# Scan and mixture of experts on one core: the first three chunks emitted whole before the weights, weight loads in ScalarE's DMA queue

## The chip, the cores and the metric

The kernel runs on one core of one Trainium2 chip. A core has TensorE (matmuls, PE in the profile; its weight loads are PEld), VectorE (DVE), ScalarE (ACT), GpSimd (POOL) and SyncE (SP, which here only issues DMAs), and 16 DMA engines that move data between HBM and the on-chip memory. Each engine works through its own stream of instructions in order; a "q" behind the engine's name marks what its sequencer does, such as issuing a DMA. The metric is the time of one execution on the device in microseconds (us), taken as the median over runs.

## The reference

A gated linear recurrence runs along each sequence, and its output goes through a mixture of experts in which each token takes one expert:

```
sig = 1 / (1 + exp(-f_logit));  f = lower_bound + (1 - lower_bound) * sig
h = f[:, t] * h + (1 - f[:, t]) * x[:, t];  y[:, t] = h        # t = 0 .. S-1
logits = y @ w_gate;   e_idx = argmax(logits);   gate_w = softmax(logits)[e_idx]
eom = 1 / (1 + exp(-(y @ w_output_gate)))
out = gate_w * eom[e_idx] * (relu(y @ w1[e_idx]) @ w2[e_idx])
```

Batch 4, sequence 5056 (20224 tokens), width 256, 8 experts, inner width 1024, float32 in and out.

## The kernel before

*Chunks.* The tokens go through the recurrence in 40 chunks of 512, channels on the partitions. `load_chunk` brings a chunk's two inputs (512 KB each) in by DMA from SP (L250, L251). `chunk` is a generator: tanh on ACT (L265), a product on DVE (L269), a scale on ACT (L274), the scan on DVE (L280), squares on ACT (L287) and a small matmul (L291) for a power-of-two scale (`pow2`), the scaled result split into two f16 halves (ACT L310, DVE L314), four DMA transposes from SP to token rows (`turn`, L307), the gate matmuls, about two dozen small DVE operations for expert, position and factor (the last is L430), and four indirect DMAs on POOL (L433) that scatter the rows into a scratch in HBM, sorted by expert. A bare `yield` ends a segment of a chunk; there are 16 of them. Within a segment, `yield SMALL` and `yield BIG` let `together` interleave the DVE work of several generators. Chunks 0 and 3 borrow memory of the weight tables of the last two experts (`lent`), the others share two buffers. `loading` wraps the generator and, at its fifth segment, issues the load of the next chunk.

*Weights.* Each of 8 experts has two halves (w1 and w2): 16 half-experts j = 0 to 15. `prep_load(j)` brings one in by two DMAs of 512 KB (L566); a matmul with itself (`prep_gram`, L578), DVE's norm (L585), a small matmul and `pow2` give a scale; ACT makes the high f16 half (`prep_hi`, L614) and DVE the low one (`prep_lo`, L619). Eight buffers hold four half-experts; the load for a later j waits until its buffer is free.

*Early tiles.* While weights are prepared, tiles of 128 tokens already run through experts that are ready. `plan_first` makes a table for one tile per expert once 3 chunks are done, and again at 5 (`EARLY`). `early(j)`, called twice a step, gathers such a tile (`gather`: a DMA transpose of the rows L630 and a small DMA L633, both on SP) and runs half of it: first matmuls (L719 to L721), relu on ACT (L723), low half on DVE (L730), second matmuls (L739 to L741), scaling on ACT (L750) and the indirect DMA of the output (L754). An expert's tile is gathered at step j = 2e + 1 at the earliest, and one tile is in work at a time.

*Order.* The loop over j = -2 to 15 emits all this; `step(k)` runs k pumps on average. A `pump` begins a chunk when `prog["tick"]` has run down, then runs one segment of each live chunk together with the step's other work and one plan. The pumps of a step are FILL = 12 for j = -2 and -1, PUMPS0 = 3 for j = 0 to 2, and PUMPS = 2.25 after. Chunks 0, 1 and 2 begin 3 pumps apart (`GAPS`), the later ones 8 (`PERIOD`). After j = 15 a closing loop (DRAIN = 1.25 pumps an iteration) runs until all 16 early tiles are through. Then come the main tiles of 256 tokens (`experts`, L675 to L677 and L706 to L708), four pumps each; a main tile copies its expert's weights on DVE (L657, L663), and its table comes from `plan` (L486 to L555). Behind 64 such tiles come single blocks of 128 tokens.
The streams of DVE, ACT, PE and POOL up to the first main tile are put in order by the compiler's scheduler, which takes the order of emission as priority; SP's stream, and every stream behind that point (`ordered`), stays as emitted.

Of the kernel before, what the change touches and what calls it, by code (L numbers as in the profile page):

```python
# [26 lines left out]
TX = 8  # L27
PERIOD = 8
PUMPS = 2.25
FILL = 12  # L30
MORE = (18, 21)
EARLY = (3, 5)
LOADAT = 5
GAPS = (3, 3)
PUMPS0 = 3.0
TURN = 3
XB = 2
# [3 lines left out]
LEAD = 2  # L41
# [4 lines left out]
def raw(ins):  # L46
    return getattr(ins, "ins", ins)
# [3 lines left out]
def tile_scan_moe(  # L51
# [10 lines left out]
    nc = tc.nc  # L62
    P = 128
# [8 lines left out]
    NCH = -(-N // CH)  # L72
    R = N + P
    FREE = E * R
# [3 lines left out]
    WH = WE // 2  # L78
    QH = WH // 2
# [4 lines left out]
    def sure(tokens):  # L84

        return max(0, -(-(tokens - len(EARLY) * E * P - E * 255) // 256))
# [8 lines left out]
    scr = dp.tile([E * R + P, RW], I16, name="scr")  # L95
# [8 lines left out]
        out=tri, in_=ones, compare_op=ALU.is_gt, fill=0.0, base=0, pattern=[[1, P]], channel_multiplier=-1  # L104
# [48 lines left out]
    def together(tasks):  # L153

        at = {id(g): (g, next(g, None)) for g in tasks}
        last = None
        while True:
            todo = [(g, kind) for g, kind in at.values() if kind]
            if not todo:
                return  # L160
            best = [x for x in todo if x[1] == SMALL and x[0] is not last]
            best = best or [x for x in todo if x[1] == BIG] or todo
            g = best[0][0]
            last = g if best[0][1] == SMALL else None
            del at[id(g)]
            at[id(g)] = (g, next(g, None))

    def alone(g):
# [12 lines left out]
        out=gsq, in0=wgf, scalar=1.0, in1=wgf, op0=ALU.mult, op1=ALU.mult, accum_out=gss  # L181
# [9 lines left out]
        out=wgs[:, :, 1, :], in0=wgc, scalar=gsc, in1=wgs[:, :, 0, :], op0=ALU.mult, op1=ALU.subtract  # L191
# [3 lines left out]
    fresh = []  # L195

    def apart(ins, group, keep=()):
        tc.declare_no_dep(raw(ins), group=group, keep=[raw(k) for k in keep], reason="rows apart")
        tc.add_to_no_dep_group(group, raw(ins))
# [8 lines left out]
    padt = cp.tile([P, RW], I16, name="padt")  # L208
    nc.gpsimd.memset(padt, 0)
    nc.gpsimd.iota(padt[:, CM + 2 : CM + 4].bitcast(I32), pattern=[[0, 1]], base=N, channel_multiplier=0)  # L210
    fresh.append(nc.sync.dma_start(out=scr[FREE : FREE + P, :], in_=padt))
    apart(fresh[0], "scr")
    row2 = [cp.tile([P, NB, RW], I16, name=f"rows{i}") for i in range(2)]

    top1 = w1f[:, (E - 1) * 2 * WH : E * 2 * WH]
# [16 lines left out]
    def beside(n=None):  # L232
        for _ in range(len(queue) if n is None else min(n, len(queue))):
            f, a = queue.pop(0)
            f(*a)
# [5 lines left out]
    def load_chunk(c):  # L241
        t0 = c * CH
        n = min(CH, N - t0)
        if c in lent:
            fx = lent[c].bitcast(F32).rearrange("p (i k n) -> p i k n", i=2, k=KD)
            ft, xt = fx[:, 0], fx[:, 1]
        else:
            ft = p1.tile([P, KD, CH], F32, tag="ft", name="ft", bufs=XB)
            xt = p1.tile([P, KD, CH], F32, tag="xt", name="xt", bufs=XB)
        nc.sync.dma_start(out=ft[:, :, 0:n], in_=fv_in[:, :, t0 : t0 + n])  # L250
        nc.sync.dma_start(out=xt[:, :, 0:n], in_=xv_in[:, :, t0 : t0 + n])  # L251
        loaded[c] = (xt, ft)
# [309 lines left out]
    def prep_load(j):  # L562
        ws = []
        for i in range(2):
            w = wp.tile([P, QH], F32, tag="w", name="w")
            nc.sync.dma_start(out=w, in_=wT[j // 2][:, j % 2 * WH + i * QH : j % 2 * WH + (i + 1) * QH])  # L566
            ws.append(w)
        half[j] = dict(w=ws)

# [46 lines left out]
    def prep_lo(j, z):  # L616
        (h, r), (l, _) = parts(j, 0, z), parts(j, 1, z)
        yield BIG
        nc.vector.scalar_tensor_tensor(out=l, in0=r, scalar=half[j]["sc"], in1=h, op0=ALU.mult, op1=ALU.subtract)  # L619
# [141 lines left out]
    prog = {"begun": 0, "tick": 0, "done": 0, "left": 0.0, "planned": 0, "final": False, "got": 0, "rounds": 0}  # L761
# [7 lines left out]
    def loading(c):  # L769

        at = 0
        for kind in chunk(c):
            if not kind:
                at += 1
                if at == LOADAT and EARLY[0] <= c + 1 < NCH:
                    load_chunk(c + 1)
            yield kind

    def plans(need):
        c = prog["done"]  # L780
        if prog["final"]:
            return
        while prog["rounds"] < len(EARLY) and c >= min(EARLY[prog["rounds"]], NCH):
            prog["rounds"] += 1
            planning.append(plan_first())
        k = sure(min(N, c * CH)) - prog["planned"]
        if k >= need or (k > 0 and c == NCH):
            prog["planned"] += k
            planning.append(plan(k, 2, False))
        if c == NCH:  # L790
            prog["final"] = True
            planning.append(plan(tail, 1, True))

    def pump(tasks, need):

        beside()
        if prog["tick"] <= 0 and prog["begun"] < NCH:
            live.append(loading(prog["begun"]))
            prog["tick"] = GAPS[prog["begun"]] if prog["begun"] < len(GAPS) else PERIOD
            prog["begun"] += 1  # L800
        prog["tick"] -= 1
        mine = planning[:1]
        del planning[:1]
        together([*live, *tasks, *mine])
        for g in [g for g in live if g.gi_frame is None]:
            live.remove(g)
            prog["done"] += 1
        plans(need)

    def step(k, tasks, need=PLAN):  # L810
        prog["left"] += k
        if prog["left"] < 1.0:
            together(tasks)
        while prog["left"] >= 1.0:
            prog["left"] -= 1.0
            pump(tasks, need)
            tasks = []
# [62 lines left out]
            prep_load(n - 1)  # L880
    for n in range(min(EARLY[0], NCH) - 1, deep):
        prep_load(n)
    for j in range(-2, nh):
        tasks = []
        if 1 <= j < nh + 1 - deep:
            prep_load(j - 1 + deep)
        if 0 <= j + 1 < nh:
            tasks.append(prep_scale(j + 1))
        for z in range(2):
            if 0 <= j:  # L890
                tasks.append(prep_lo(j, z))
            mine, rest = early(j)
            tasks += mine
            step((PUMPS if j >= TURN else PUMPS0 if j >= 0 else FILL) / 2, tasks, LEAD)
            if 0 <= j + 1 < nh:
                prep_hi(j + 1, z)
            rest()
            tasks = []
            if j + 2 < nh:
                if z == 0:  # L900
                    prep_gram(j + 2)
                    tasks.append(prep_norm(j + 2))
                else:
                    prep_sum(j + 2)
# [110 lines left out]
```

## Time and profile before

| | |
|---|---|
| median of 3 runs | 1020.92 us (1020.44 to 1021.68) |
| the profiled execution: its time, its span | 1019.5 us, 1017.8 us |
| busy PE, DVE, ACT, POOL | 917.6 (90%), 886.5 (87%), 511.8 (50%), 378.2 (37%) us |
| first arithmetic on a chunk on DVE | 9.06 us |
| first matmul of an early tile (L719) | 61.5 us |
| last low half of a weight (L619) begins | 149.62 us |
| first matmul of a main tile (L675) | 185.4 us |
| mean granted clock of TensorE | 0.989 |

In a row in order of time the columns are start, duration, engine, line, operation, output <- inputs, shape, count; in brackets stands how long the engine had been idle and what ended that. A row of waits names the waiting engine and line, what it waited for, and total, number and longest of these waits. A row of the table by stages has the stretch, its length, then for each engine its busy time and number of instructions, the granted clock, the DMA engines' share, and GB/s.

### The profile page before, as it was taken

How to read it: one execution, taken by the hardware profiler on the slowest of the kernel's cores; microseconds unless marked ns; L12 is line 12 of the kernel's file. 1: busy time of each engine (PE TensorE's matmuls, PEld its weight loads, DVE VectorE, ACT ScalarE, POOL GpSimd, SP SyncE). 2: the span in 40 equal slices, each digit the busy share in tenths (PEclk: the TensorE clock that was granted, in tenths of full speed). 3: DMA queues.
4: the chain of work that ended last, by engine and by line, in shares of the span. 5: the costliest groups of instructions: out<-in, count | busy, mean ns of one | idle time of the engine just before them, and what ended most of it. 6: DMA issues, size and time to landing. Idle time of an engine off the chain costs nothing. (4 is left out here: it accounts for less than half of the span.)

```text
span 1017.8 us, 27499 instructions
## 1 busy us (share of the span) xinstructions
PE 917.6 (90%) x9775; PEld 822.5 (81%) x9775; DVE 886.5 (87%) x2803; ACT 511.8 (50%) x1075; POOL 378.2 (37%) x378
## 2 busy tenths in 40 slices
PE   2267998899999999999999999999999999999993
PEld 2156987788888888888888888888888888899993
DVE  7889897899999999999999999999999998758771
ACT  5667684554554555545545455455455543333331
POOL 1532334334344443433444434344444344221121
PEclk9999999999999999999999999999999999999997
DMA  8899976755655556456566555565565644321120
GB/s 311 200 305 271 254 179 147 163 154 137 139 136 151 145 136 163 135 136 142 132 141 156 157 147 133 136 139 132 142 154 135 151 91 97 97 54 43 43 55 16
DMA packets 238546, 146.34 MB, mean 144 GB/s; under 512 B 202557, under 2 KB 204223, under 8 KB 238400
## 3 DMA queue, kind: packets, MB, share of 16 engines
q1 hardware_dynamic: 222752, 101.74, 43.5%
q0 software_dynamic: 15360, 42.74, 13.3%
q8 instruction: 80, 1.31, 0.6%
q14 instruction: 66, 0.54, 0.2%
q10 hardware_dynamic: 288, 0.02, 0.0%
HBM read 58.38 MB, written 44.49 MB: 101 GB/s over the span
## 5 line engine op out<-in xcount | busy, mean ns | idle before, releaser
L675 PE MATMUL ph<-xq,w 128*128 128x256 f16 (+1 forms) x1312 | 331.0, 261 | 3.2 <-DMA xq<-scr 2.7
L677 PE MATMUL ph<-xq,w 128*128 128x256 f16 (+1 forms) x1312 | 331.6, 261 | 0.0
L676 PE MATMUL ph<-xq,w 128*128 128x256 f16 (+1 forms) x1312 | 331.3, 261 | 0.0
L706 PE MATMUL py<-w,hh 128*128 128x256 f16 x1168 | 318.0, 272 | 10.4 <-DVE w L663 5.5
L708 PE MATMUL py<-w,hl 128*128 128x256 f16 x1168 | 318.3, 273 | 0.0
L707 PE MATMUL py<-w,hh 128*128 128x256 f16 x1168 | 318.2, 272 | 0.0
L754 POOL DMA_INDIRECT out_dram<-yo,mt x146 | 165.9, 1137 | 298.4 <-ACT yo L750 270.5
L433 POOL DMA_INDIRECT scr<-rows,dst x154 | 178.9, 1162 | 225.3 <-issue 212.5
L680 ACT ACTIVATE hh<-ph 128x512 f16<-128x512 f32 (+1 forms) x328 | 178.7, 545 | 156.9 <-PE ph L677 154.9
L688 DVE SCALAR_TENSOR_TENSOR hl<-ph,hh 128x512 f16<-128x512 f32 (+1 forms) x328 | 204.8, 625 | 10.4 <-ACT hh L680 8.6
L675 PEld LDWEIGHTS <-w 128*128 128x128 f16 x1312 | 128.0, 98 | 16.5 <-DVE xt L269 3.0
L677 PEld LDWEIGHTS <-w 128*128 128x128 f16 x1312 | 128.1, 98 | 12.1
L657 DVE COPY w<-w1s 128x2048 f16 x164 | 114.9, 701 | 26.2 <-PE ph L677 24.7
L676 PEld LDWEIGHTS <-w 128*128 128x128 f16 x1312 | 127.9, 97 | 9.7
L707 PEld LDWEIGHTS <-hh 128*128 128x128 f16 x1168 | 113.9, 98 | 23.2 <-issue 12.7
L708 PEld LDWEIGHTS <-hl 128*128 128x128 f16 x1168 | 113.9, 98 | 13.5
L706 PEld LDWEIGHTS <-hh 128*128 128x128 f16 x1168 | 113.9, 98 | 11.2
L663 DVE COPY w<-w2s 128x2048 f16 x164 | 111.9, 682 | 0.5 <-PE py L708 0.3
L274 ACT ACTIVATE ft<-ft,fb,fa 128x512 f32<-128x512 f32 (+1 forms) x76 | 60.6, 807 | 97.9 <-DVE xt L269 90.1
L310 ACT ACTIVATE ft<-xt,sa 128x512 f16<-128x512 f32 (+1 forms) x76 | 50.2, 708 | 104.9 <-DVE li L299 100.7
L280 DVE TENSOR_TENSOR_SCAN xt<-ft,xt 128x512 f32<-128x512 f32 (+4 forms) x78 | 90.9, 1173 | 0.0
L750 ACT ACTIVATE yo<-py,fac 128x256 f32<-128x256 f32 x146 | 61.5, 465 | 26.4 <-PE py L708 22.8
(172 smaller groups left out, 1355.0 us busy)
## 6 DMA issues: line engine op xcount, KB each, us to landing
ft<-in_fT_dram SPq DMA_DIRECT2D x37, 512.0 KB
xt<-in_xT_dram SPq DMA_DIRECT2D x37, 512.0 KB
w<-in_wT_dram SPq DMA_DIRECT2D x32, 512.0 KB
scr<-rows,dst POOLq DMA_INDIRECT x154, 2.8
rows<-ft SPq DMA_TRANSPOSE x152
out_dram<-yo,mt POOLq DMA_INDIRECT x146, 2.4
xq<-scr SPq DMA_TRANSPOSE x99
scr<-padt SPq DMA_DIRECT2D x9, 136.0 KB
```

Source lines behind the costliest of these rows:

```text
L433: ins = nc.gpsimd.indirect_dma_start(out=scr[:, :], out_offset=IOA(ap=dst[:, b : b + 1], axis=0), in_=rows[:, b, :], in_offset=None)
L657: nc.vector.tensor_copy(out=w, in_=w1f[:, ds(T["ev"] * (2 * WH) + h * 2 * QH, 2 * QH)])
L663: nc.vector.tensor_copy(out=w, in_=w2f[:, ds(T["ev"] * (2 * WH) + h * 2 * QH, 2 * QH)])
L675: nc.tensor.matmul(out=o, lhsT=w[:, f, k, 0, :], rhs=T["xh"][:, k, 0:n], start=first, stop=False)
L676: nc.tensor.matmul(out=o, lhsT=w[:, f, k, 0, :], rhs=T["xl"][:, k, 0:n], start=False, stop=False)
L677: nc.tensor.matmul(out=o, lhsT=w[:, f, k, 1, :], rhs=T["xh"][:, k, 0:n], start=False, stop=last)
L680: nc.scalar.activation(hh[:, :, 0:n], ph[:, :, 0:n], AF.Relu)
L688: nc.vector.scalar_tensor_tensor(out=hl[:, :, 0:n], in0=ph[:, :, 0:n], scalar=0.0, in1=hh[:, :, 0:n], op0=ALU.max, op1=ALU.subtract)
L706: nc.tensor.matmul(out=o, lhsT=hh[:, i, c], rhs=w[:, f, 0, :], start=first, stop=False, skip_group_check=True)
L707: nc.tensor.matmul(out=o, lhsT=hh[:, i, c], rhs=w[:, f, 1, :], start=False, stop=False, skip_group_check=True)
L708: nc.tensor.matmul(out=o, lhsT=hl[:, i, c], rhs=w[:, f, 0, :], start=False, stop=last, skip_group_check=True)
L754: ins = nc.gpsimd.indirect_dma_start(out=out[:, :], out_offset=IOA(ap=T["mt"][:, b, 2:4].bitcast(I32), axis=0), in_=T["yo"][:, b, :], in_o ...
```

## The change

Four edits. Chunks 0, 1 and 2 are emitted whole, one after the other, before the loop over j; the two steps that ran 12 pumps now run one each, and chunk 3 begins with the first pump. The weight loads are issued from ScalarE's queue instead of SP's. The store of the padding rows goes from the front of SP's queue to behind the first loads. The constants GAPS and FILL go.

```diff
-FILL = 12
-GAPS = (3, 3)
+GAP = 0
...
-    fresh.append(nc.sync.dma_start(out=scr[FREE : FREE + P, :], in_=padt))
-    apart(fresh[0], "scr")
     row2 = [cp.tile([P, NB, RW], I16, name=f"rows{i}") for i in range(2)]
...
             w = wp.tile([P, QH], F32, tag="w", name="w")
-            nc.sync.dma_start(out=w, in_=wT[j // 2][:, j % 2 * WH + i * QH : j % 2 * WH + (i + 1) * QH])
+            nc.scalar.dma_start(out=w, in_=wT[j // 2][:, j % 2 * WH + i * QH : j % 2 * WH + (i + 1) * QH])
...
             live.append(loading(prog["begun"]))
-            prog["tick"] = GAPS[prog["begun"]] if prog["begun"] < len(GAPS) else PERIOD
+            prog["tick"] = PERIOD
             prog["begun"] += 1
...
     for n in range(min(EARLY[0], NCH) - 1, deep):
         prep_load(n)
+    fresh.append(nc.sync.dma_start(out=scr[FREE : FREE + P, :], in_=padt))
+    apart(fresh[0], "scr")
+
+    for n in range(min(EARLY[0], NCH)):
+        prog["begun"] += 1
+        for kind in loading(n):
+            pass
+        prog["done"] += 1
+        plans(LEAD)
+    prog["tick"] = GAP
     for j in range(-2, nh):
...
-            step((PUMPS if j >= TURN else PUMPS0 if j >= 0 else FILL) / 2, tasks, LEAD)
+            step((PUMPS if j >= TURN else PUMPS0 if j >= 0 else 1) / 2, tasks, LEAD)
```

## The prediction

> **What bounds the kernel now.** I read the page, then a table of the engines by stage, then each engine in order of time, then the waits. The page's slices say where time can be had: the middle is full, the first seven slices (25 us each) are not alike.
>
> ```profile
> span 1017.8 us, 27499 instructions
> ...
> DVE  7889897899999999999999999999999998758771
> ```
>
> The table has stages cut at events: first chunk arithmetic (9 us), first matmul of an early tile (61.5), end of weight preparation (151), first main tile (185.4), one-block tiles (899). Columns: PE, PEld, DVE, ACT, POOL busy, granted clock, DMA share, GB/s.
>
> ```profile
> 9.00:41.00 32.00, 11.43 (x137) 9.36 (x136) 30.91 (x127) 22.38 (x47) 5.71 (x5) 1.00 1.05 296
> 41.00:61.50 20.50, 2.90 (x41) 1.90 (x42) 17.36 (x56) 15.11 (x26) 9.28 (x10) 1.00 0.81 237
> 61.50:151.00 89.50, 78.53 (x1101) 73.82 (x1101) 78.07 (x256) 62.01 (x105) 29.41 (x30) 0.98 0.99 254
> 151.00:185.40 34.40, 29.32 (x376) 26.60 (x373) 25.84 (x96) 17.66 (x38) 14.59 (x14) 0.95 0.60 136
> 185.40:899.00 713.60, 693.29 (x6769) 614.50 (x6770) 654.08 (x2092) 354.06 (x764) 293.27 (x278) 1.00 0.56 137
> ```
>
> From 185.4 on PE is 97% busy: that part is PE's and the diff removes no matmul. Before it DVE is 97% busy to 41 us, 85% to 61.5, 87% to 151, beside a DMA share near 1; PE has little to do until 61.5. So the change can only move the moment 185.4, and what moves it is DVE work and queues ahead of it.
>
> **What holds the first early tile.** In time order, SP's queue:
>
> ```profile
> 3.16 0.38 SPq L211 DMA_DIRECT2D scr<-padt  x1
> 3.60 0.42 SPq L250 DMA_DIRECT2D w2s<-in_fT_dram  x1
> ...
> 46.20 5.17 SPq L307 DMA_TRANSPOSE rows<-w1s  x4
> ...
> 52.59 1.69 SPq L566 DMA_DIRECT2D w<-in_wT_dram  x2
> 56.06 1.21 SPq L630 DMA_TRANSPOSE xq<-scr  x1
> ```
> ```profile
> 61.50 0.26 PE L719 MATMUL ph<-xq,w1s 128*128 128x128 f16 x1 [2.92 <-DMA xq<-scr]
> ```
> ```profile
> 9.06 1.29 DVE L269 SCALAR_TENSOR_TENSOR w2s<-w2s 128x512 f32<-128x512 f32 x2 [3.68 <-DMA w2s<-in_xT_dram]
> ...
> 40.68 0.22 DVE L430 TENSOR_SCALAR rows<-fc,xi 128x4 f32<-128x4 f32 x1
> ...
> 149.62 1.28 DVE L619 SCALAR_TENSOR_TENSOR w2s<-w,ws,w2s 128x1024 f16<-128x1024 f32 x1
> ```
> ```profile
> 51.22 0.96 POOL L433 DMA_INDIRECT scr<-rows,dst  x1 [0.30 <-issue]
> ```
> ```profile
> DMA to landing us min/median/max: 2.5/2.9/3.5
> ```
>
> Chunk 2's last DVE instruction is at 40.68, the last of its scatters starts on POOL at 51.22 and lands about 2.9 us after its end (the landing row is L433's), at 55.1; the gather follows at 56.06, behind chunk 3's four transposes and a pair of weight loads on SP, and its rows release PE at 61.50. DVE did the three chunks in 31.8 us, of it some 7.9 on other work (weight half 0: two L619 of 1.28; chunk 3: two scans of 1.28, two L269 of 0.65, and about 1.5 of small ones): **8.0 us of DVE per chunk**.
>
> **The change, by count of the code.** A chunk has 17 segments (16 bare yields and the end); a pump runs one segment of each live chunk. Before: 24 pumps in j = -2 and -1 (FILL 12 twice), chunks 0, 1, 2 begun at pumps 0, 3, 6, chunk 3 at 14, then one each 8; 3 pumps a step for j = 0 to 2, 2.25 after: 62 pumps at the end of j = 15. After: chunks 0 to 2 whole, chunk 3 begun at pump 0, one each 8; 1+1+9+29.25 = 40 pumps at the end of j = 15. Chunk segments emitted by then: before 7x17+16+8 = 143, after 6x17+16+8 = 126. **Exactly one chunk (17 segments) leaves the weight stage**, all of it ahead of j = 2, where the first early tile sits. It is done later, among main tiles.
> The second round of early tiles needs five chunks: pump 38 before (j = 5, gathers at j = 6, 8, ... 14), pump 24 after (j = 8, gathers at j = 10, 12, 14). So **two early tiles move behind j = 15**: the closing loop takes 2x4+3 = 11 iterations before, 2x6+3 = 15 after.
>
> **Costs, step by step.**
>
> *Start.* SP no longer waits for POOL's memsets: the 3.60 load can go some 2.5 us earlier. Against it, eight weight loads sit in ACT's queue ahead of the first tanh.
>
> ```profile
> 1.71 1.28 ACT L265 ACT_TABLE_LOAD   x1 [1.71 <-PEq L1004]
> 7.66 1.15 ACT L265 ACTIVATE w2s<-w2s 128x512 f32<-128x512 f32 x2 [4.67 <-DMA w2s<-in_fT_dram]
> ```
> ```profile
> L566 SPq DMA_DIRECT2D w<-in_wT_dram x32: 328/390/1102, 5.6 to 125.7; - x32
> ```
>
> 8 x 0.39 = 3.1 us (8.8 at the slowest issue) from 1.71, and the table load: tanh can start at 6.1, at worst 11.8, against 7.66. Ends -2 and +4; I take -0.5: by the median issue tanh goes 1.6 earlier, and sharing the engines (rival 4) takes most of that back. The padding rows' own store is needed only by the first gather, 50 us on: nothing.
> The loads now go out from two queues at once, where all moved at 296 GB/s in 9 to 41 us. The Trainium skill, "DMA: Bandwidth & Descriptors", Queues, rings and completion order, says each DMA engine alternates between queue rows packet by packet; Issuing engines are not separate DMA queues adds that a second issuer buys no bandwidth. By that, chunk loads get half the rate at the start; the trace, with one queue, cannot show it (rival 4).
>
> *To the first early tile.* One chunk less: -8.0. The chain agrees: three chunks of DVE from 8.5 us (24 us) with 4 to 7 us of weight work slipped between end at 36 to 40; four scatters and landing (about 8) 44 to 48; gather and landing as now (61.5 - 56.06 = 5.4): 50 to 53.5 instead of 61.5. The ends are -4 (chains of dependent small operations stay uncovered) and -12; I take -8.0. SP's transposes of chunk 3 (5.2 us) and weight loads (1.7) go behind the gather; they are not added, as the scatter landing ends last.
>
> *j = 2 to 15 (89.5 us).* Two tiles less:
>
> ```profile
> L730 DVE SCALAR_TENSOR_TENSOR el<-ph,eh 128x512 f16<-128x512 f32 x32 | 21.8, 686 | 3.2 <-ACT eh L723 3.1
> ...
> L649 DVE TENSOR_SCALAR fac<-mt,cinv 128x1 f32<-128x1 f32 x16 | 3.4, 210 | 8.2 <-DMA mt<-scr 8.1
> ```
> 2 x (2x0.686+0.21) = 3.2 us of DVE, at 87% busy 3.7. SP also loses 24 weight loads (24 x 0.39 = 9.4 us) and their waits:
> ```profile
> SPq L566 <- DVE w1s L619: 3.3, 2, 2.0
> ...
> SPq L566 <- DVE xv L146: 0.3, 1, 0.3
> ```
> These are the longest and the shortest of ten such rows, 12.3 us in all, each a time in which gathers and chunk transposes stood behind a load that waited for a buffer. PE waited for gathers, DVE for their small half (8.1 us, above):
> ```profile
> PE ph L719 <- DMA xq<-scr: 13.0, 7, 3.3
> ```
> I give a third of DVE's 8.1 us, -2.5 (ends 0 and -8). The loads land on ACT, which has 27.5 us free of 89.5: 9.4 us of issue fit. I cost that at nothing; what hides it is ACT's idle time, and without it the price is 9.4 + 12.3 = 21.7 us. Behind a waiting load stand ACT's tanh, high halves and relus, and DVE and PE behind those. Sum of the stage: -6.2.
>
> *Closing loop.* 34.4 us for 11 iterations, of which one gather wait:
> ```profile
> 165.10 0.23 PE L719 MATMUL ph<-xq,w1s 128*128 128x128 f16 x1 [3.30 <-DMA xq<-scr]
> ```
> (34.4-3.3)/11 = 2.83 us; PE alone 29.32/11 = 2.67. Four more iterations: +10.5, ends +10 and +12.5 (3.13 each, stall and all).
>
> *Main.* Chunk segments done at its start: 173 before (pump 76), 167 after (pump 59): a third of a chunk more in 713.6 us, nothing on PE but its few gate matmuls. The lead shrinks: between a chunk's last segment and the plan that uses it lie 6 pumps before, 3 after.
> ```profile
> 407.81 0.16 DVE L486 TENSOR_TENSOR pl_n<-cnt,boff 128x8 f32<-128x8 f32 x1
> ...
> 415.58 0.23 DVE L430 TENSOR_SCALAR rows<-fc,xi 128x4 f32<-128x4 f32 x1
> ```
> ```profile
> 420.94 1.49 POOL L433 DMA_INDIRECT scr<-rows,dst  x1 [0.30 <-issue]
> ```
> ```profile
> 433.90 1.26 SPq L630 DMA_TRANSPOSE xq<-scr  x1
> ```
> The period is 22.5 us (8 pumps of 2.8). The gather comes 18.3 us after L430; the rows have landed at 420.94+1.49+2.9 = 425.3, after 9.7. Three pumps less: 9.9. Just enough; 0, at worst +3.
>
> **Sum:** -0.5 -8.0 -6.2 +10.5 = -4.2 us. The profiled execution took 1019.5 (span 1017.8 and 1.7 around it): 1015.3; the median of the runs stands 1.4 higher, so 1020.9 - 4.2 = **1016.7**.
>
> **Rivals.**
> 1. *Slower: ACT becomes the bound of the weight stage.* Of the 21.7 us that move to its in-order queue more than 6.3 stay uncovered (4.2 gained, and 2.1 more). For: ACT is 74% busy in 41 to 61.5, and one waiting load holds all kinds of work. Against: 32.9 us free on ACT from 41 to 151. At half uncovered, +10.8: 1027.5; at the point where it decides, 1023. Chance 0.17.
> 2. *A wash: the stage only trades.* The scheduler, which reorders DVE freely here, fills chunk chains with weights as it does now, so little starts sooner, no SP relief, and an iteration costs 3.13: -0.5-8.0-3.7+12.5 = +0.3: 1021.2. For: PE's work before 185.4 stays the same, tiles only change place. Chance 0.20.
> 3. *A larger gain: SP was the real hold.* All of the 8.1 us of DVE's waits go and the closing loop's 3.3 us stall with them: -4.2 -5.6 -3.3 = -13: 1007.8. For: the gathers' waits above; against: a DMA share of 0.99 delays a gather wherever it is issued. Chance 0.18.
> 4. *The weights crowd the chunk loads.* Chunk 0's 1.05 MB takes 3.5 us alone at 296 GB/s, 7.1 at half rate: +3.5 on the first arithmetic: 1020.2. For: the DMA share is above 1 in 9 to 41 us already; against: SP starts 2.5 us sooner, and DVE has chunks 0 and 1 to do before it needs chunk 2. Chance 0.05. The rule for it is the one of the Trainium skill's page named under *Start*; no row of this trace bears it out or denies it.
>
> The forecast has 0.40. A measurement tells 0.2% (2.0 us) from no change. Faster: 0.37 of the forecast, rival 3, and a little of 2: 0.58. Same: most of 2, part of 4 and of the forecast: 0.21. Slower: 0.21. The range takes in rival 3's end and rival 1's decision point: 1007.5 to 1024; the forecast's own is 1013 to 1019.
>
> **What would show it.** First L719 at 50 to 54 us; last L619 near 136 us; first L675 near 181 us; SP's gathers with no L566 between; ACT's idle time ended by L566 short. Last L619 near 150, with ACT waiting at L566, is rival 1; a gap over 48 us from there to L675, rival 2; x0 later than 9.06, rival 4; waits of L675 for xq through the middle would mean the lead was needed.

## The result, and the profile after

The changed kernel takes 1079.35 us (median of 4 runs, 1077.42 to 1081.33) against 1020.68 us for the kernel before on the same chip (4 runs, 1020.25 to 1021.68): 1.0573 times, 95% interval 1.0552 to 1.0595. It is slower by 58.7 us where the prediction had 4.2 us faster. The profiled execution took 1077.4 us with a span of 1075.7, against 1019.5 and 1017.8. Lines of the changed kernel's code are three lower than before from the dropped lines on (L716 is what L719 was).

The page of the changed kernel (span; busy tenths in 40 slices of 27 us):

```profile
span 1075.7 us, 27421 instructions
...
PE   1218668869999999999999999999999999989993
...
DVE  4668867569999999999999999999999999747772
```

Its table by stages: the same stretch of 9 to 41 us, then cut at its own events as before (first early tile, end of the last low half of a weight, first main tile), and about as long a stretch of main tiles:

```profile
9.00:41.00 32.00, 9.57 (x104) 7.70 (x104) 19.21 (x61) 16.82 (x34) 3.30 (x4) 1.00 0.55 191
41.00:77.30 36.30, 2.56 (x30) 1.52 (x31) 25.86 (x93) 19.60 (x32) 10.19 (x11) 1.00 0.86 213
77.30:171.70 94.40, 69.36 (x955) 65.50 (x955) 73.00 (x250) 57.69 (x95) 23.54 (x22) 0.89 0.88 207
171.70:228.70 57.00, 41.25 (x557) 36.51 (x555) 35.56 (x124) 24.39 (x53) 22.87 (x23) 0.95 0.54 133
228.70:942.00 713.30, 678.80 (x6685) 605.88 (x6685) 659.81 (x2092) 361.02 (x763) 275.14 (x274) 1.00 0.58 136
```

The events in their rows (ACT's queue and first tanh; PE; DVE; PE again):

```profile
1.76 14.73 ACTq L563 DMA_DIRECT2D w<-in_wT_dram  x8
16.52 1.28 ACT L262 ACT_TABLE_LOAD   x1 [16.52 <-DMA ft<-in_fT_dram]
17.82 1.15 ACT L262 ACTIVATE w2s<-w2s 128x512 f32<-128x512 f32 x2
```
```profile
77.28 0.27 PE L716 MATMUL ph<-xq,w1s 128*128 128x128 f16 x1 [12.54 <-DMA xq<-scr]
```
```profile
170.44 1.28 DVE L616 SCALAR_TENSOR_TENSOR w2s<-w,ws,w2s 128x1024 f16<-128x1024 f32 x1
```
```profile
228.66 0.37 PE L672 MATMUL ph<-xq,w 128*128 128x256 f16 x1 [8.04 <-DMA xq<-scr]
```

The first of these rows merges eight issues and the pauses between them. One issue is short (ns: shortest, median, longest):

```profile
L563 ACTq DMA_DIRECT2D w<-in_wT_dram x32: 334/334/513, 1.8 to 134.8; - x32
```

So of the 14.73 us that the first eight take, the larger part is pauses (the longest from 8.2 to 13.9 us), in which ACT's queue does not come to the tanh behind it. The row of the table load names the chunk's input as the releaser, but chunk 0's two inputs had landed by 4.0 and 5.6 us (the ends of their packets in the trace; 6.8 and 8.2 before). It was ACT's queue that held the tanh.

| us | before | after | lost in the stage |
|---|---|---|---|
| first tanh on ACT | 7.7 | 17.8 | 10.2 |
| first early tile | 61.5 | 77.3 | 5.6 |
| last low half of a weight | 149.6 | 170.4 | 5.0 |
| first main tile | 185.4 | 228.7 | 22.4 |
| end of the span | 1017.8 | 1075.7 | 14.6 |

Nothing got faster and no single place holds the loss. The number to see in the table by stages is DVE's: 19.2 us busy of the stretch 9 to 41, where it had 30.9; then 71%, 77% and 62% of the three stages up to the main tiles, where it had 85%, 87% and 75%. DVE's work did shrink in the weight stage (73.0 us instead of 78.1, where 3.2 us less had been counted for two early tiles); its idle time rose from 11.4 to 21.4. PE stands for gathers, in the stretch 60 to 230:

```profile
PE ph L716 <- DMA xq<-scr: 35.0, 5, 12.8
...
PE ph L672 <- DMA xq<-scr: 8.0, 1, 8.0
```

against 13.0 us in seven waits before (60 to 190). And the main tiles have a wait that was not there. The waits of PE in 300 to 900 us, after, and the same wait in the kernel before:

```profile
PE pv L288 <- ACT ft L284: 30.4, 26, 1.6
```
```profile
PE pv L291 <- ACT ft L287: 0.4, 2, 0.2
```

### The profile page after: what moved, and what is told of

The parts are those of the page before. It is cut to its first block, busy times and chain, and to the rows that moved or that the text cites. A ratio compares the mean times of both kernels' runs of the same rounds, so it can differ in the third digit from the quotient of the medians.

```text
span 1075.7 us, 27421 instructions
## 1 busy us (share of the span) xinstructions
PE 915.7 (85%) x9775; PEld 823.4 (77%) x9775; DVE 898.0 (83%) x2803; ACT 520.1 (48%) x1075; POOL 362.9 (34%) x378
## 3 DMA queue, kind: packets, MB, share of 16 engines
q0 software_dynamic: 15360, 42.74, 12.7%
## 5 line engine op out<-in xcount | busy, mean ns | idle before, releaser
L672 PE MATMUL ph<-xq,w 128*128 128x256 f16 (+1 forms) x1312 | 332.0, 262 | 12.7 <-DMA xq<-scr 12.7
L430 POOL DMA_INDIRECT scr<-rows,dst x154 | 170.4, 1106 | 418.9 <-issue 408.4
L751 POOL DMA_INDIRECT out_dram<-yo,mt x146 | 160.4, 1099 | 152.6 <-ACT yo L747 116.2
L674 PEld LDWEIGHTS <-w 128*128 128x128 f16 x1312 | 128.4, 98 | 12.4
L673 PEld LDWEIGHTS <-w 128*128 128x128 f16 x1312 | 128.4, 98 | 10.2
L284 ACT ACTIVATE ft<-xt 128x512 f32<-128x512 f32 (+1 forms) x76 | 47.4, 625 | 91.5 <-DVE xt L277 89.0
L716 PE MATMUL ph<-xq,w1s 128*128 128x128 f16 x256 | 48.8, 230 | 35.0 <-DMA xq<-scr 35.0
```

Of the source, the lines that this page charges most:

```text
L430: ins = nc.gpsimd.indirect_dma_start(out=scr[:, :], out_offset=IOA(ap=dst[:, b : b + 1], axis=0), in_=rows[:, b, :], in_offset=None)
L672: nc.tensor.matmul(out=o, lhsT=w[:, f, k, 0, :], rhs=T["xh"][:, k, 0:n], start=first, stop=False)
L673: nc.tensor.matmul(out=o, lhsT=w[:, f, k, 0, :], rhs=T["xl"][:, k, 0:n], start=False, stop=False)
L674: nc.tensor.matmul(out=o, lhsT=w[:, f, k, 1, :], rhs=T["xh"][:, k, 0:n], start=False, stop=last)
L751: ins = nc.gpsimd.indirect_dma_start(out=out[:, :], out_offset=IOA(ap=T["mt"][:, b, 2:4].bitcast(I32), axis=0), in_=T["yo"][:, b, :], in_o ...
```

## The experiments

All ratios are to the kernel before on the same chip. The same kernel before took 1019.6 to 1020.7 us on four of the chips and 1028.4 and 1029.7 us on two others, so runs of different sets are compared by ratio, and absolute times only within a set; that holds for the times of the stages too, which are some us longer on the slower chips (the sets of pad_re and ord_pad), and for the microseconds that the expectations name. Every run in one table (us; "main tiles" is from their first matmul to the end of the span; runs between rules shared a chip). The edits and written orders shift lines, so the same instruction has other line numbers in other runs: the first matmul of an early tile, L719 before, is L716 after, L724 in pad_re and L727 in act24_re.

| run | ratio, 95% interval | first tanh | first early tile | last low half | first main tile | main tiles |
|---|---|---|---|---|---|---|
| before | 1 | 7.7 | 61.5 | 149.6 | 185.4 | 832.4 |
| after | 1.0573 (1.0552 to 1.0595) | 17.8 | 77.3 | 170.4 | 228.7 | 847.0 |
| — | | | | | | |
| act_only | 1.0367 (1.0326 to 1.0409) | 20.1 | 81.3 | 192.5 | 230.4 | 832.7 |
| loads_sp | 1.0426 (1.0404 to 1.0449) | 4.6 | 57.6 | 159.5 | 214.2 | 848.6 |
| eight_sp | 1.0478 (1.0452 to 1.0504) | 4.6 | 62.3 | 159.2 | 217.7 | 848.8 |
| ten_pumps | 1.0436 (1.0417 to 1.0454) | 18.2 | 80.1 | 196.7 | 234.6 | 833.8 |
| — | | | | | | |
| ten_sp | 1.0167 (1.0144 to 1.0190) | 4.5 | 64.0 | 163.3 | 201.5 | 832.5 |
| late_pv | 1.0484 (1.0448 to 1.0521) | 17.9 | 74.5 | 167.4 | 227.2 | 838.8 |
| pad_act24 | 1.0255 (1.0232 to 1.0278) | 4.5 | 60.9 | 175.5 | 213.7 | 832.6 |
| pad_only | 1.0130 (1.0086 to 1.0174) | 4.5 | 58.7 | 154.4 | 192.7 | 834.5 |
| — | | | | | | |
| pad_re | 0.9979 (0.9958 to 1.0001) | 4.5 | 58.5 | 151.7 | 191.5 | 835.9 |
| act_re | 1.0192 (1.0151 to 1.0233) | 20.0 | 72.3 | 167.7 | 205.3 | 836.5 |
| act24_re | 1.0067 (1.0042 to 1.0092) | 4.6 | 63.4 | 162.8 | 202.2 | 835.3 |
| c3_re | 1.0050 (1.0029 to 1.0070) | 4.7 | 61.0 | 158.3 | 195.5 | 835.3 |
| — | | | | | | |
| ord_pad | 1.0081 (1.0061 to 1.0102) | 7.7 | 61.4 | 160.7 | 197.9 | 836.0 |
| ord_act | 1.0285 (1.0263 to 1.0306) | 7.5 | 75.1 | 184.6 | 219.5 | 835.5 |
| c3_two | 1.0676 (1.0637 to 1.0715) | 4.5 | 55.5 | 158.1 | 212.5 | 884.6 |
| c3_free | 1.0164 (1.0145 to 1.0183) | 4.9 | 61.6 | 164.6 | 204.7 | 836.1 |
| — | | | | | | |
| loads_sp_b | 1.0404 (1.0370 to 1.0437) | 4.7 | 56.8 | 156.1 | 209.3 | 847.5 |
| c3_two_b | 1.0341 (1.0310 to 1.0373) | 4.8 | 52.6 | 152.7 | 206.0 | 848.7 |

### Which edit costs: queue, order of the chunks, missing pumps

*act_only*, the kernel before with all weight loads on ACT:

```diff
-            nc.sync.dma_start(out=w, in_=wT[j // 2][...
+            nc.scalar.dma_start(out=w, in_=wT[j // 2][...
```

> The kernel before with one edit: weight loads issued from ACT. Theory 1 (ACT's first tanh stands behind eight load issues, about 10 us at the start, and that is all the queue costs): first tanh near 17 us, time 1031, 1026 to 1036. Rival 2 (the in-order ACT queue holds up the whole weight stage): 1045 or more, and ACT idle time ended by the loads' waits after 60 us. Rival 3 (the order of the chunks alone is to blame): 1019 to 1024.

1059.0 us. One word of the diff costs 37 thousandths. The eight loads keep ACT's queue until 18.8 us, though no issue took over 0.45 us:

```profile
1.72 17.10 ACTq L566 DMA_DIRECT2D w<-in_wT_dram  x8
```

But the blocked start is 12.4 us and the first main tile is 45 us late. The time is that of rival 2, its sign is not: the later loads on ACT wait for no buffer (their semaphore waits take 0.017 us each). What the rest is was open here.

*loads_sp* and *eight_sp*, the changed kernel with all loads, or the first eight, back in SP's queue:

```diff
-            nc.scalar.dma_start(out=w, in_=wT[j // 2][...
+            nc.sync.dma_start(out=w, in_=wT[j // 2][...
```
```diff
-            nc.scalar.dma_start(out=w, in_=wT[j // 2][...
+            (nc.sync if j < WPB // 2 else nc.scalar).dma_start(out=w, in_=wT[j // 2][...
```

> The changed kernel with its weight loads back on SP's queue, chunks still first. Theory 1: the start comes back (tanh near 5 to 8 us), the rest stays: 1069, 1063 to 1073. Rival 2: nearly all comes back, 1035 or less. Rival 3: 1074 or more, nothing comes back.

> The changed kernel with only the first eight weight loads on SP, the other 24 on ACT. Theory 1: the same as with all loads on SP, 1069 (1063 to 1073), since only the eight at the start stand ahead of work. Rival 2: between, 1055 to 1060 if the later loads matter as much as the first. Rival 3: 1074 or more.

1064.6 and 1069.2 us. With no load on ACT the rest of the change (whole chunks, missing pumps, padding rows later) still costs 43 thousandths; with the loads on ACT it is 15 more, and two thirds of these 15 come with the first eight loads. Each of these kernels also has its own order of instructions on the four engines, which turns out below to matter, so such differences are not prices of the edit alone.

*ten_pumps*, the changed kernel with ten pumps instead of two in j = -2 and -1 (11 closing iterations and six pumps from a chunk's end to its plan, as before):

```diff
-            step((PUMPS if j >= TURN else PUMPS0 if j >= 0 else 1) / 2, tasks, LEAD)
+            step((PUMPS if j >= TURN else PUMPS0 if j >= 0 else 5) / 2, tasks, LEAD)
```

> The changed kernel with ten pumps (five a step) in j = -2 and -1 instead of two, so that chunk progress beside the weights is as in the kernel before: closing loop 11 iterations instead of 15, 6 pumps of lead instead of 3. Theory 1 (the deferred chunk costs two early tiles in the closing loop, about 13 us, the lead at the first main tile, 8 us, and 14.7 us of PE waits through the main tiles): 1044, 1036 to 1052. Rival 2 (queue): 1070 or more. Rival 3 (chunks one behind the other leave DVE idle): 1060 to 1075, the main tiles back to 832 us but the start no sooner.

1065.5 us: main tiles back from 847.0 to 833.8 us, the first of them no sooner, as rival 3 had it. In all runs but late_pv the main tiles take 847 to 849 us with two pumps and 832 to 835 with ten or with the pumps of before (on the two slower chips 835 to 837, and once, with two pumps, 885; below).

*ten_sp*, both together: loads on SP and ten pumps.

> The changed kernel with the weight loads back in SP's queue and ten pumps instead of two in j = -2 and -1, so that the later chunks get back the pumps that the change took from them (11 closing iterations again, six pumps from a chunk's end to its plan). What is left of the change is the order alone: three whole chunks, then weights. Theory A, the missing pumps cost it: main tiles start near 186 and take 833 us as before, 1015 to 1025 us in all. Theory B, three chunks one behind the other leave DVE dry and the weight stage then runs on gathers that come late: main tiles 833 us, but the first of them at 200 to 220 us, 1035 to 1055 us in all.

1036.6 us, as theory B put it. Of the 43 thousandths of loads_sp, 26 go with the missing pumps: 16 us of main tiles and 12.7 us of their start. 17 are left for three whole chunks ahead of the weights, the moved padding rows and the order that came with them.

### Where the main tiles lose 15 us

*late_pv*, the changed kernel with a pump more in front of the squares' matmul:

```diff
+        if between["on"]:
+            yield
         pv = pp.tile([P, 1], F32, tag="rw", name="pv")
```

> The changed kernel, with one more empty segment in front of a chunk's matmul of the squares (pv) once the main tiles run, so that the plan's small DVE operations, which now stand just ahead of the scan, have a pump more before PE stands at that matmul. Theory P, the 15 us that the main tiles lost are PE standing at that matmul behind late squares: main tiles back from 847 to between 833 and 838 us, 1065 to 1070 us in all, and the wait of pv for ACT's squares (30 us in 26 pieces) gone. Theory L, the loss is the shorter lead of the plan and the gathers: main tiles stay at 845 to 850 us, 1077 to 1081 us in all.

1068.8 us; main tiles 838.8 us. With three pumps from a chunk's end to its plan, the plan's twenty small DVE operations, 3.7 us, stand right ahead of another chunk's scan. In the changed kernel's DVE rows:

```profile
498.14 0.15 DVE L483 TENSOR_TENSOR pl_n<-cnt,boff 128x8 f32<-128x8 f32 x1
...
501.78 0.17 DVE L552 SCALAR_TENSOR_TENSOR pl_done<-pl_done 128x8 f32<-128x8 f32 x1
501.87 1.28 DVE L277 TENSOR_TENSOR_SCAN xt<-ft,xt 128x512 f32<-128x512 f32 x1
...
504.25 1.27 DVE L277 TENSOR_TENSOR_SCAN xt<-ft,xt 128x512 f32<-128x512 f32 x1
```

The squares on ACT and the matmul on PE behind them come that much later, and PE, in order, stands:

```profile
506.39 0.16 PE L288 MATMUL pv<-hss,na 128*128 128x1 bf16 x1 [1.17 <-ACT ft L284]
```

26 of these make the 30 us above, of which 15 are lost. In late_pv that wait is gone, but now PE stands longer for a weight copy on DVE. Waits of PE in 300 to 900 us, late_pv and, for the same matmul, the kernel before:

```profile
PE py L705 <- DVE w L662: 22.9, 25, 1.3
```
```profile
PE py L706 <- DVE w L663: 5.1, 13, 0.4
```

So theory P holds for 8 us of the 15 (838.8 is just above its 833 to 838); the other 6 came back at the next place where PE hangs on DVE.

### What the queue costs beside the blocked start

*pad_act24*, the kernel before with 24 loads on ACT and the padding rows stored later; *pad_only*, with the padding rows alone:

```diff
-            nc.sync.dma_start(out=w, in_=wT[j // 2][...
+            (nc.sync if j < WPB // 2 else nc.scalar).dma_start(out=w, in_=wT[j // 2][...
```
```diff
-    fresh.append(nc.sync.dma_start(out=scr[FREE : FREE + P, :], in_=padt))
-    apart(fresh[0], "scr")
...
     for n in range(min(EARLY[0], NCH) - 1, deep):
         prep_load(n)
+    fresh.append(nc.sync.dma_start(out=scr[FREE : FREE + P, :], in_=padt))
+    apart(fresh[0], "scr")
```

> The kernel before, with the first eight weight loads still in SP's queue, the other 24 in ScalarE's, and the padding rows stored behind the first loads. Theory Q1, only the first eight hurt, because they stand ahead of the first tanh: first tanh near 4.6 us, 1016 to 1024 us in all. Theory Q2, weight loads on ScalarE hurt all through the weight stage, because the scheduler may put them earlier there than SP's written order did and they then crowd the gathers: first tanh near 4.6 us, main tiles not before 205 us, 1040 to 1050 us in all.

> The kernel before, with only the store of the padding rows moved behind the first loads. All theories: first tanh near 4.6 instead of 7.7 us. If the early start is kept, 1015 to 1019 us; if the order of DVE and the gathers set the first early tile anyway, 1019 to 1022 us. Above 1025 us it would show that an edit that moves nothing else upsets the written order of the weight stage.

1046.0 and 1030.6 us. pad_only, an edit that delays one store of 136 KB and nothing else, starts tanh 3.2 us earlier and the first early tile 2.8 us earlier, and ends 13 thousandths slower. Its SP queue is the same but for that store. The streams of the other engines are not: up to the first main tile the scheduler puts them in order anew for every program. So kernels were made in which that order is written out: each engine's instructions, numbered as emitted, are chained in the order that another kernel's scheduler had chosen.

```diff
+ORDER = {
...
+    def replay(cut):
+        for name, runs in ORDER.items():
+            mine = [i for i in nc.cur_bb.bb.instructions[:cut] if i.engine == getattr(nc, name).engine]
+            line = []
+            for r in runs.split():
+                a, n = (int(v) for v in (r + "+1").split("+")[:2])
+                line += mine[a : a + n]
...
+            for a, b in zip(line[:-1], line[1:]):
+                tc.add_manual_dep(b, a.name, AFTER, reason="order")
```

*pad_re*: pad_only with the order of the kernel before. *ord_pad*: the kernel before with the order of pad_only.

> The kernel before, with the store of the padding rows behind the first loads as in pad_only, but with the order of the instructions on PE, DVE, ACT and POOL ahead of the main tiles written out exactly as in the kernel before. Only SP's queue differs. Theory W, what pad_only lost (11 us) came from the new order that the scheduler wrote on the four engines, not from the moved store: 1015 to 1021 us, and first main tile no later than 186 us. Theory D, the loss comes from the moved store or the earlier loads themselves: 1027 to 1033 us again.

> The kernel before, unchanged in what it issues and in SP's queue, but PE, DVE, ACT and POOL follow ahead of the main tiles the order that the scheduler wrote for pad_only. The mirror of pad_re. Theory W, the order is what pad_only lost by: 1.010 to 1.018 times the kernel before, first main tile 6 to 10 us late. Theory D: 0.998 to 1.003.

0.9979 and 1.0081. With the old order the moved store gains 2 us (the interval just reaches 1); with the new order and the store where it was, 8 thousandths are lost. So the order costs, from both sides. Its price in ord_pad lies below theory W's 1.010 to 1.018, and the two ratios together make 6 of pad_only's 13 thousandths; the three runs were on three chips, and the rest stays open.

*act_re*: act_only with the order of before; the later 24 loads stand on ACT where SP had issued them in time. *act24_re*: the same with the first eight on SP and the padding rows later. *ord_act*: the kernel before, loads on SP, with the order of act_only.

```diff
+PLACE = [0, 0, 0, 0, 0, 0, 0, 0, 54, 54, 60, 60, 69, 69, 72, 73, 74, 76, 84, 84, 94, 95, 99, 99, 101, 103, 115, 116, 126, 126, 128, 129]
...
+            for m, k in zip(moved[::-1], PLACE[::-1]):
+                line.insert(k + 2, m)
```

> The kernel before with all 32 weight loads in ScalarE's queue (act_only), but with the order on PE, DVE, POOL and of all else on ACT kept as in the kernel before, and each of the later 24 loads put on ACT behind as many instructions as had started when SP issued it before. Theory W, of act_only's 39 us only the blocked start belongs to the queue, the rest to the newly written order: first tanh near 20 us, main tiles from 195 to 202 us, 1030 to 1037 us in all. Theory D, the queue itself costs all through the weight stage: main tiles from 220 us or later, 1052 to 1062 us.

> As pad_re (padding rows later, order as in the kernel before), with the later 24 weight loads on ACT behind as many instructions as had started when SP issued them before; the first eight stay in SP's queue. Theory W: 1014 to 1022 us, the 24 issues on ACT (0.33 us each) hidden in its idle time. Theory D: 1040 to 1048 us, as pad_act24.

> The kernel before, all loads in SP's queue as ever, but PE, DVE, POOL and all else on ACT follow the order that the scheduler wrote for act_only. Theory W, half of act_only's loss (37 thousandths, of which 19 stayed when the order was put back) is that order alone: 1.013 to 1.025 times the kernel before. Theory D, that order is only bad together with late first loads: 0.998 to 1.006.

1.0192, 1.0067 and 1.0285. The order of act_only, without a load on ACT, costs 28 thousandths; the loads on ACT, with the old order, 19. The two do not add up to act_only's 37. One reason stands in ord_act's DVE rows:

```profile
14.99 0.29 DVE L592 SCALAR_TENSOR_TENSOR jk<-pg,ident 128x128 f16<-128x128 f32 x1 [9.60 <-PE pg L585]
...
15.21 1.29 DVE L276 SCALAR_TENSOR_TENSOR w2s<-w2s 128x512 f32<-128x512 f32 x2
```

That order puts a weight's norm ahead of the first product of chunk 0. In act_only the weight was there first, and the norm ran at 8.40 us; with the loads on SP, DVE waits 9.6 us for it, and the product comes at 15.21 instead of 9.06. So ord_act shows what an order can cost that does not fit the loads, above theory W's 1.013 to 1.025, and not what this order costs inside act_only. act_re, which would be 1039 us where the kernel before takes 1020, lies above theory W's 1030 to 1037: the queue costs more than its blocked start. act24_re would be 1027 us, between theory W's 1014 to 1022 and theory D's 1040 to 1048; against pad_re on the same chip it shows 9 thousandths for 24 loads of 0.33 us each (median) that wait for nothing. Its rows about the first early tile, ACT's queue, SP's queue and PE:

```profile
55.38 0.34 ACTq L574 DMA_DIRECT2D w<-in_wT_dram  x1
...
57.53 0.34 ACTq L574 DMA_DIRECT2D w<-in_wT_dram  x1
```
```profile
55.90 1.21 SPq L638 DMA_TRANSPOSE xq<-scr  x1
```
```profile
63.41 0.26 PE L727 MATMUL ph<-xq,w1s 128*128 128x128 f16 x1 [7.14 <-DMA xq<-scr]
```

and the same in pad_re:

```profile
53.39 1.24 SPq L635 DMA_TRANSPOSE xq<-scr  x1
54.84 0.42 SPq L638 DMA_DIRECT2D mt<-scr  x1
55.40 0.81 SPq L571 DMA_DIRECT2D w<-in_wT_dram  x2
```
```profile
58.54 0.27 PE L724 MATMUL ph<-xq,w1s 128*128 128x128 f16 x1 [2.62 <-DMA xq<-scr]
```

With one queue, the second pair of loads stands behind the gather (55.40 behind 53.39), and the gather's rows are there after 5.2 us. With two, the load of 55.38 is out ahead of the gather, the next one follows at 57.53, and the same gather takes 7.5 us. It also started 2.5 us later, because the scatters ahead of it landed later: POOL's wait for them was 5.9 us instead of 3.7, with loads of the second queue in flight. The queue that the change relieved had been what kept the loads behind the gather. The changed kernel has the same picture at its first gather, SP's queue and ACT's:

```profile
67.58 1.21 SPq L627 DMA_TRANSPOSE xq<-scr  x1
```
```profile
66.69 0.33 ACTq L563 DMA_DIRECT2D w<-in_wT_dram  x1
...
67.95 0.35 ACTq L563 DMA_DIRECT2D w<-in_wT_dram  x1
```

Its rows release PE at 77.28, after 9.7 us, where the gather of 56.06 before took 5.4.

### What three whole chunks cost

In loads_sp DVE does almost nothing from 32 to 37 us. Its rows in loads_sp_b, and SP's queue beside them:

```profile
30.99 1.41 DVE L311 SCALAR_TENSOR_TENSOR ft<-xt,sa,ft 128x512 f16<-128x512 f32 x2 [0.66 <-ACT ft L307]
36.71 1.29 DVE L266 SCALAR_TENSOR_TENSOR w1s<-w1s 128x512 f32<-128x512 f32 x2 [4.30 <-DMA w1s<-in_xT_dram]
37.92 0.22 DVE L342 TENSOR_TENSOR lgo<-lgp 128x64 f32<-128x64 f32 x1
```
```profile
24.62 6.08 SPq L304 DMA_TRANSPOSE rows<-ft  x4
30.75 0.59 SPq L247 DMA_DIRECT2D w1s<-in_fT_dram  x1
31.39 0.50 SPq L248 DMA_DIRECT2D w1s<-in_xT_dram  x1
```

The product of chunk 3 stands ahead of chunk 2's small operations (L342 and on), and waits 4.3 us for chunk 3's inputs (5.5 us in ten_sp, where the row names an operation on ACT instead; c3_re below tests it). SP issues these only at 30.75, behind the eight transposes of chunks 0 and 1. Chunk 2's last scatter, and with it the first gather, hangs on that. The changed kernel has the wait too:

```profile
48.59 1.29 DVE L266 SCALAR_TENSOR_TENSOR w1s<-w1s 128x512 f32<-128x512 f32 x2 [4.05 <-DMA w1s<-in_xT_dram]
...
55.83 0.23 DVE L427 TENSOR_SCALAR rows<-fc,xi 128x4 f32<-128x4 f32 x1
```

*c3_re* is ten_sp, and *c3_two* loads_sp, each with its order kept and chunk 3's loads put up front; *c3_free* has the edits of c3_re and an order of the scheduler's own.

```diff
-                if at == LOADAT and EARLY[0] <= c + 1 < NCH:
+                if at == LOADAT and EARLY[0] < c + 1 < NCH:
...
     for n in range(min(EARLY[0], NCH) - 1, deep):
         prep_load(n)
+    load_chunk(EARLY[0])
```

> ten_sp (three whole chunks first, loads in SP's queue, ten pumps) with its order on PE, DVE, ACT and POOL kept exactly, and chunk 3's two input loads put up front in SP's queue, behind the first eight weight loads, instead of behind the transposes of chunks 0 and 1. Theory C, DVE stood 5.5 us at chunk 3's product, which had been written ahead of chunk 2's last fifteen small operations, for a load that SP had not yet issued; that held the first early tile: it comes at 57 to 60 instead of 64 us, 1030 to 1034 us in all. Rival: the gather is held by something else (the scatters, the transposes on SP): first early tile at 62 to 65 us, 1035 to 1038 us.

> The changed kernel with the loads in SP's queue (loads_sp), its order kept exactly, and chunk 3's two input loads up front as in c3_re; still two pumps in j = -2 and -1. Theory C, the wait for chunk 3 at 32 to 37.7 us was on the chain of this one too: first early tile 3 to 6 us earlier than 57.6, 1.032 to 1.038 times the kernel before against loads_sp's 1.0426; what is left is the missing pumps (four more closing iterations and 15 us of main tiles). Rival: the first early tile comes earlier, but the second round's gathers are as late as before: 1.040 to 1.045.

> The same edits as c3_re (three whole chunks, ten pumps, loads in SP's queue, chunk 3 loaded up front), but with the order left to the scheduler. If the scheduler's order for it is as good as the kept one: 1.000 to 1.006 times the kernel before; if a newly written order costs what it cost in pad_only: 1.010 to 1.020. Under 0.998 this would be the version that beats the kernel before.

c3_re: 1.0050, against 1.0167 for ten_sp on another chip; 12 thousandths from two DMAs, more than the 5.5 us of the wait. Its first early tile, 61.0 us on the slower chip, is not quite at theory C's 57 to 60. c3_free: 1.0164; the same edits with an order newly written lose all of that again. c3_two gave no answer: its first early tile came 2.1 us before that of loads_sp, where 3 to 6 had been expected, but its main tiles took 885 us on one of the slower chips. PE has many short gaps there that nothing in the profile explains, 37 us of them in 300 to 900 us, the most at the gate matmuls:

```profile
PE pr L333 <- issue: 14.4, 25, 1.1
```

*loads_sp_b* and *c3_two_b* are the same two kernels once more, on one chip.

> loads_sp once more, on one chip with c3_two_b, since c3_two lost 36 us in its main tiles on another chip than loads_sp had run on. If the short lead of two pumps is what tips over on that chip: main tiles at 880 us or more here too, 1.060 to 1.070 times the kernel before. If it is not the chip: main tiles 846 to 852 us, 1.040 to 1.046.

> c3_two once more, beside loads_sp_b. If c3_two's 884 us of main tiles belong to this kernel: 1.062 to 1.072 times the kernel before again, whatever chip it is. If they came with the chip: loads_sp_b shows them as well, or neither does, and c3_two_b stands 3 to 6 us below loads_sp_b.

1.0404 and 1.0341: chunk 3's loads up front gain 5.3 us (1060.4 to 1055.1) with two pumps as well. Its DVE rows have no gap, and its first early tile comes at 52.6 us:

```profile
30.95 1.41 DVE L318 SCALAR_TENSOR_TENSOR ft<-xt,sa,ft 128x512 f16<-128x512 f32 x2 [0.66 <-ACT ft L314]
32.29 1.28 DVE L273 SCALAR_TENSOR_TENSOR w1s<-w1s 128x512 f32<-128x512 f32 x2
33.49 0.22 DVE L349 TENSOR_TENSOR lgo<-lgp 128x64 f32<-128x64 f32 x1
```

So the 885 us came with that chip, and of the four kernels run there to this one alone: c3_free and the two order runs, with six pumps from a chunk's end to its plan, took 836 us on it. That a lead of three pumps leaves less room on a slower chip would fit; it is not shown.

## Why the prediction was wrong, step by step

**Start, -0.5; measured +10.2.** The step "8 x 0.39 = 3.1 us" failed. The price of one issue was right (0.33 to 0.51 us on ACT); what the sum left out is the pauses between issues when several 512 KB loads stand in a row. Eight took 14.73 us, and even the bound (8 x 1.10, tanh at 11.8) fell short of 17.8. The trace of the kernel before had it, in SP's queue (each row from a narrow window, since a wider one merges them):

```profile
11.45 0.33 SPq L566 DMA_DIRECT2D w<-in_wT_dram  x1
12.75 0.33 SPq L566 DMA_DIRECT2D w<-in_wT_dram  x1
14.01 0.33 SPq L566 DMA_DIRECT2D w<-in_wT_dram  x1
```

Issues of 0.33 us stand 1.3 us apart, which for 512 KB is 410 GB/s, about what moved then (416, below). Rival 4 named the crowding and priced it at 3.5 us, on the chunk loads. Its sign, first arithmetic later than 9.06 us, was seen (18.48), but chunk 0's inputs landed earlier than before; what tanh waited for was the issuing engine. The Trainium skill ("DMA: Bandwidth & Descriptors", Issuing engines are not separate DMA queues) has a second issuer add no bandwidth. That agrees with the rows of 10 to 20 us, before and after, last column GB/s:

```profile
10.00:20.00 10.00, 2.60 (x21) 1.96 (x20) 9.06 (x24) 8.79 (x19) 0.00 (x0) 1.00 1.04 416
115.00:135.00 20.00, 17.99 (x260) 16.83 (x259) 17.12 (x58) 14.21 (x24) 8.41 (x9) 1.00 1.03 266
```
```profile
10.00:20.00 10.00, 1.91 (x16) 1.49 (x15) 1.52 (x3) 3.46 (x6) 0.00 (x0) 1.00 1.04 415
```

416 and 415 GB/s, while DVE's busy time (fifth number) fell from 9.06 to 1.52. The second row of the first view is used at the end. The same section adds that a second issuer saves the time to initiate a DMA. Here that time, pauses and all, went to an engine that had work to do.

**To the first early tile, -8.0; measured +5.6 behind the late start.** What failed is that three chunks run without holes. From the first product to chunk 2's last operation DVE took 37.4 us (18.48 to 55.83) where it had taken 31.6: a fourth chunk's product stood in between, and waited 4.1 us for a load that SP had behind transposes. The prediction let "chains of dependent small operations" cost 4 of the 8 us at worst, and did not ask what the next chunk's load does to them. POOL made up for most of it: the last scatter ended 10.4 us later than before, which is the late start and hardly more. The other 5.4 us came behind it: 1.1 until the gather, and 4.3 by which the gather took longer, with weight loads from the second queue beside it (and chunk 3's transposes behind it, as in pad_re). So "gather and landing as now" failed as well. The count of DVE work is not contradicted: with loads on SP and chunk 3 loaded in time the tile came at 52.6, inside the forecast 50 to 53.5 (c3_two_b; the same kernel had 55.5 on a slower chip).

**j = 2 to 15, -6.2; measured +5.0.** Less DVE work, but 10 us more idle time. The step "a third of DVE's 8.1 us" as a gain failed: relief of SP's queue let the loads out ahead of the gathers (act24_re), and the order on DVE and PE was a new one. Rival 2 said that the scheduler reorders DVE freely, and took it for a wash; its sign, over 48 us from the last low half to the first main tile, was seen (58.2). That a new order can be no wash is what pad_re and ord_pad show, with 8 thousandths; ord_act has 28, with an order that does not fit its loads.

**Closing loop, +10.5; measured +22.4.** The count holds: five early tiles are gathered behind the last low half instead of three. But by the table by stages fifteen iterations take 3.8 us each instead of 2.83; PE is busy 41.3 of 57.0 us. The step that failed is the rate, taken over from a loop in which the first main tile's gather was in time. One wait of 8.0 us for that gather is new: it went out at 224.68, when the scatters of the chunk ahead had just landed. Without it an iteration takes 3.3 us; the rest of the misjudged rate was not taken apart.

**Main, 0, at worst +3; measured +14.6.** The gathers were in time, as argued ("just enough"). The step that failed is "nothing on PE but its few gate matmuls": three pumps instead of six also moved the plan's DVE work to a place where a matmul of PE hangs on it.

**Rival 1** had the sign but not the cause: no load on ACT waited for a buffer (semaphore waits of 0.017 us), and ACT was busy 61% of the weight stage. It priced the queue as 21.7 us spread over the stage; the block is 15 us at the start.

In all, from 57 thousandths down: loads back to SP 15, ten pumps 26, chunk 3's loads in time 12 (order kept, other chip), and 5 are left. The first two steps each brought a newly written order with them, so the parts are differences between kernels. How much of these 57 is the order newly written for the changed kernel is not known, since no kernel has its emission and a proven order. No version tried beats the kernel before by more than the 2 us of pad_re.

## What to carry to other kernels

Where a scheduler writes the order of several engines, every edit ahead of it is two edits; price the second by keeping the old order (pad_re) and by giving the old kernel the new one (ord_pad), before explaining a loss by the edit itself. A DMA queue is also an order: the loads that shared it with the gathers went out behind them, and those that left it did not. A sum of issue times leaves out the pauses between issues, so read the pace of a queue from the starts of its rows. And when work is moved later by a few steps, look for what it now stands in front of, as well as for what may come too late.

## What the runs showed of the hardware

Eight loads of 512 KB in a row keep ACT's queue for 14.7 to 17.1 us, though one issue takes 0.33 to 0.51 us (after; 0.45 at most in act_only); between them the queue pauses, without a wait that the profile names. In SP's queue before, the pauses made 1.3 us from issue to issue, about the pace of the transfers. On ACT, with the chunk loads in SP's queue beside them, 4.2 MB in 14.73 us is 285 GB/s of the 415 that moved; that the queue pauses until transfers ahead are done would fit, and is not shown. A late gather costs PE its clock as well: in eight_sp, where PE stood 11.6 us for one, it was busy 5.2 of 20 us and its granted clock (third number from the end) fell to 0.59; the same stretch before, shown above, has 18.0 us and 1.00.

```profile
115.00:135.00 20.00, 5.24 (x55) 4.89 (x53) 12.16 (x51) 9.00 (x13) 8.07 (x8) 0.59 0.61 202
```

That agrees with the Trainium skill, "TensorE: Matmul & The Clock Gate", Part 1, by which an idle PE is throttled and gets its clock back only after a while of work.
